# Retention and top-1 mixture of experts on one core: expert counts, ranks and table scatters at the end of the block that chose, one block's rows ahead of weight loads, squares behind the first layer

## The chip, the cores and the metric

The kernel runs on one core of a Trainium2 chip. The metric is the device time of one execution in microseconds (us). Five engines run their own instruction streams: TensorE (PE, with its weight loads as PEld), VectorE (DVE), ScalarE (ACT), GpSimd (POOL) and SyncE (SP), which here only issues DMAs.

## The reference

Two stages in a row. Retention (linear attention with a decay per head) makes 3072 token rows of 512 values; each row then goes to the one expert whose normalized embedding it matches best.

```python
# retention, B, H, S, D = 4, 8, 768, 64
for t in range(S):
    state = gamma[None, :, None, None] * state + np.einsum('bhd,bhe->bhde', k[:, :, t], v[:, :, t])
    y[:, :, t] = scale * np.einsum('bhd,bhde->bhe', q[:, :, t], state)
x = y.transpose(0, 2, 1, 3).reshape(B * S, H * D)

# top-1 experts, N, D, E, F = 3072, 512, 8, 1024
logits = xn @ en.T / tau                    # rows and embeddings divided by their norms
expert_idx = np.argmax(logits, axis=1)
gate_w = softmax(logits)[np.arange(N), expert_idx]
for e in range(E):
    mask = expert_idx == e
    h = np.maximum(x[mask] @ w1[e], 0.0)
    out[mask] = gate_w[mask, None] * (h @ w2[e])
```

## The kernel before

**Stage one** walks over 12 blocks of 256 tokens (`for m in range(NM)`, `NM = 12`). In a block PE makes scores of queries and keys (`scores`, L381), DVE masks them (`masks`, L401), PE adds the product with the carried state (`inter`) and with the values (`intra`, L445), ACT copies the result out as `yT` (`take`), and DVE turns it into token rows that SP writes to the DRAM tensor `xd` (`rows`, L472 and L479). GpSimd scales the keys and queries of the block after next (`scale_k`, L344 and `scale_q`, L339; two instructions each). PE turns them for the next block (L350, L368).

**The choice of expert** is made for groups of blocks, `GROUPS = ((0,1,2),(3,4,5),(6,7),(8,),(9,10),(11,))`, in the block behind a group's last one (`done`). The steps are:

- `logits_products` and `logits_rows` (L492, L500): logits of the previous block, turned into rows;
- `sums` (PE, L510), then `choose` and `add_counts` (DVE, L520 to L550): the largest logit, the one-hot row `oh`, the running counts `cum`;
- `count` (PE, L537 to L541) and `ranks` (DVE, L557 to L561): each token's place in its expert's list, `sloti`. Behind group 3, `pad` (PE L586, DVE L587 and L589) also fills the first expert's early list up to 288 tokens;
- `place` (GpSimd, L570): one indirect DMA for 128 tokens, which scatters them into the DRAM table `tbl`.

In the code before, `count`, `ranks` and `place` of a group stand in the block behind the one that chose: `waiting = done` at a block's end, `place_ranks(waiting)` in the middle of the next block, for group 3 at the top of block 10. Scatters are handed out some to a block (`place(ready[:n])`).

**The join.** In block 10 SP reads the first 384 table entries (`early_slots`, L606, tile `tb`), and GpSimd gathers the first expert's early rows from `xd` by them (`early_gather`, L600, three indirect DMAs into `xge`). In block 11 PE turns `xge` (`turn_rows`, L617), and ACT and DVE split it into a high and a low part (`rows_T`, L624 and L625: `xh0`, `xl0`).

**Stage two** runs the eight experts. Every product is three matmuls (high x high, high x low, low x high). Weight pieces come by SP (`load_piece`, tile `raw`, four buffers), ACT makes the high part (`split_cast`, L219) and DVE the low part (`low`, L224). The first expert's first layer (96 matmuls on 288 columns, L237) is a generator: `run(n)` issues the next n, and other steps stand between such calls. Its results go through `hidden` (ACT L243, DVE L246, tiles `hh` and `hl`); the second layer (L1055) follows. `square` (ACT, L278) sums a row's squares for its gate.

**What sets the order.** All five queues run in the order in which the code issues the steps (`tc.manual_schedule`), so a step's place in the source is its place on each engine. PSUM tiles of stage one come from a ring of four banks (`pt_`): scores, logits, turned keys and queries, `sums`, `count` and `pad` take the next bank in turn, and a PE step waits until the bank's last contents have been read.

Of the kernel before, what the change touches and what calls it, by code (L numbers as in the profile page):

```python
# [28 lines left out]
NM = B * NCB  # L29
# [76 lines left out]
def retention_moe(ctx: ExitStack, tc: tile.TileContext, q, k, v, emb, tau, w1, w2, const, const16, out):  # L106
# [67 lines left out]
    def after(i, o):  # L174
        tc.add_manual_dep(i.ins, o.ins.name, SYNC, reason="pace")
# [159 lines left out]
    def scale_q(m, a, eng=nc.gpsimd):  # L335

        at = (m % NCB * 2 + a) * 8
        w = C("tq")[:, at:at + 8].unsqueeze(2).broadcast_to([P, 8, D])
        return eng.tensor_tensor(out=qs_r[:, m % 3, :, a], in0=qin[m % 3][:, a], in1=w, op=ALU.mult)  # L339
# [427 lines left out]
    waiting, ready = None, []  # L767

    def scale_ahead(m, i):
        if m + 2 < NM:  # L770
            for s in range(2):
                after(scale_k(m + 2, s), i)
            for s in range(2):
                after(scale_q(m + 2, s), i)

    def place_ranks(g):
        pr = count(g)
        run_all(ranks(g, pr))
        if span(g).stop == NBE:
            pad()  # L780
        ready.extend(range(span(g).start, span(g).stop))

    for m in range(NM):
        nxt = m + 1 < NM
        done = last_of.get(m - 1)
        if m == NM - 2:
            place_ranks(waiting)
# [12 lines left out]
        n = 2 if m < 7 else 3 if m < 8 else 4  # L800
        if m == NM - 2:
            place(ready)
            del ready[:]
# [10 lines left out]
        if m == NM - 3:  # L814
            load_piece()
            load_piece()
# [25 lines left out]
        else:  # L842
# [10 lines left out]
            if waiting is not None and m < NM - 2:  # L853
                place_ranks(waiting)
            place(ready[:n])
            del ready[:n]
            logits_rows(m - 1, logits_products(m - 1))
            if nxt:
# [15 lines left out]
                rows(m - 1, gathered if m == NM - 2 else None)  # L874
# [10 lines left out]
                intra(m, 1)  # L885
            else:
                intra(m, 0)
# [3 lines left out]
                for low in lows:  # L891
                    low()
                intra(m, 1)
                pr = count(done)
                ps = [turn_rows(xge, EROWS, kt, bank(f"pst{kt}")) for kt in range(2)]
                run_all(ranks(done, pr))
                place(range(span(done).start, span(done).stop))
        waiting = done
# [10 lines left out]
        if m == NM - 1:  # L909
            for kt in range(KT):  # L910
                rows_T(xge, EROWS, kt, slice(0, EARLY), ps[kt] if kt < 2 else None)

# [33 lines left out]
    run(11)  # L946
# [5 lines left out]
    run(21)  # L952
# [22 lines left out]
    for j, n in EROWS:  # L975
        square(xge, n, j, j)
# [4 lines left out]
    run(DF)  # L981
    ctxa.close()
# [404 lines left out]
```

## Time and profile before

| what | before |
|---|---|
| median of 3 runs | 397.76 us (397.32 to 399.26) |
| the profiled execution: its time | 396.75 us |
| the profiled execution: its span, first to last instruction | 395.0 us |
| PE busy | 384.7 us (97%) |
| DVE busy | 241.5 us (61%) |
| ACT busy | 225.6 us (57%) |
| POOL busy | 151.1 us (38%) |
| granted TensorE clock, mean | 0.997 |

Busy is the time in which an engine has an instruction running; the span is what the profile covers, and 1.8 us of the execution's time lie around it. A timeline row gives the start in us from the span's start, the time it took in us, engine, line, operation, tiles and shapes, how many instructions it merges, and in brackets the idle time before it with what ended it.

### The profile page before, as it was taken

To read this page: it belongs to the slowest core of one execution; us is meant where nothing else is said; L and a number is where in the kernel's file an instruction comes from. 1 tells how busy PE (TensorE), PEld (TensorE's weight loads), DVE (VectorE), ACT (ScalarE), POOL (GpSimd) and SP (SyncE) were. 2 spreads that over 40 slices of the span, in tenths; PEclk is the share of its full clock that TensorE was granted. 3 is DMA by queue.
4 is the path that set the end of the run, shared out by engine and by line. 5 is a ranking of instruction groups with operands and counts; after the bars stand their busy time and mean duration, and the time that the engine had idled before them with its cause. 6 is when DMAs were issued, how large, how long until landed. Compare 5 with 4: busy or idle time off the path is not lost.

```text
span 395.0 us, 9539 instructions
## 1 busy us (share of the span) xinstructions
PE 384.7 (97%) x3646; PEld 353.9 (90%) x3646; DVE 241.5 (61%) x518; ACT 225.6 (57%) x400; POOL 151.1 (38%) x171
## 2 busy tenths in 40 slices
PE   8999999999999999999999999999999999999992
PEld 4988888888879988999999999999899889999971
DVE  5565766678998569618763862865467437486300
ACT  5687787887937266537345653735755545454420
POOL 2666487788342516024402712510480161001131
PEclk9999999999999999999999999999999999999998
DMA  8999999999479788695969789696889587933121
GB/s 229 271 313 269 273 244 296 247 271 222 109 206 290 232 208 283 195 248 201 311 186 247 268 259 243 211 332 169 247 284 312 144 278 240 211 113 110 47 94 37
DMA packets 88479, 88.39 MB, mean 224 GB/s; under 512 B 10808, under 2 KB 67000, under 8 KB 88424
## 3 DMA queue, kind: packets, MB, share of 16 engines
q1 hardware_dynamic: 83176, 74.60, 67.2%
q0 software_dynamic: 5072, 13.03, 10.0%
q8 instruction: 30, 0.49, 0.5%
q14 instruction: 25, 0.20, 0.2%
q10 hardware_dynamic: 176, 0.07, 0.1%
HBM read 65.01 MB, written 18.79 MB: 212 GB/s over the span
## 4 chain that ended last, share of the span: by engine, by line
PE 91%; DVE 2%; DMA 2%; issue 2%; ACT 0%; POOL 0%; DVEq 0%; POOLq 0%; ACTq 0%
PE pst L237 12%; PE b L237 10%; PE py L1055 8%; PE py L237 8%; PE py L445 8%; PE b L381 6%; PE b L1105 6%; PE b L1055 6%; PE pst L1055 5%; PE py L1105 4%; PE b L350 3%; PE pst L415 3%; PE pst L1105 3%; PE b L368 3%; DMA raw<-in_moe_w_dram 2%
## 5 line engine op out<-in xcount | busy, mean ns | idle before, releaser
L224 DVE TENSOR_TENSOR wlo<-raw,whi 128x1024 fp32r<-128x1024 f32 x64 | 77.8, 1218 | 22.5 <-ACT whi L219 17.2
L1087 POOL DMA_INDIRECT out_dram<-og,si x28 | 29.0, 1037 | 124.4 <-ACT og L1080 58.2
L219 ACT CAST whi<-raw 128x1024 fp32r<-128x1024 f32 x64 | 66.2, 1043 | 6.6 <-DMA raw<-in_moe_w_dram 6.5
L401 DVE TENSOR_TENSOR pm<-b,mask 128x512 f32<-128x512 f32 x48 | 29.8, 684 | 18.3 <-PE b L381 18.3
L600 POOL DMA_INDIRECT xr<-xd,gi x24 | 28.9, 1206 | 17.2 <-DMA raw<-in_moe_w_dram 10.0
L1036 DVE STREAM_TRANSPOSE xt<-xg 128x384 f32<-128x384 f32 (+1 forms) x28 | 15.7, 578 | 32.0 <-DMA xg<-xs 31.9
L237 PE MATMUL pst<-xl,whi 128*128 128x380 f32 (+7 forms) x96 | 32.2, 335 | 0.0
L237 PE MATMUL pst<-xh,whi 128*128 128x380 f32 (+7 forms) x96 | 32.1, 334 | 0.0
L237 PE MATMUL pst<-xh,wlo 128*128 128x380 f32 (+7 forms) x96 | 32.0, 333 | 0.0
L344 POOL TENSOR_TENSOR hl<-wlo,cst 128x512 f32<-128x512 f32 x22 | 22.5, 1043 | 19.8 <-DMA wlo<-in_k_dram 12.8
L1037 ACT CAST xh<-xt 128x408 fp32r<-128x408 f32 (+6 forms) x28 | 14.2, 510 | 25.1 <-DVE xt L1036 24.8
L570 POOL DMA_INDIRECT tbl<-zt,sloti x24 | 23.9, 996 | 11.1 <-issue 4.8
L263 POOL TENSOR_TENSOR r<-r,half 128x4 f32<-128x4 f32 (+1 forms) x9 | 8.9, 993 | 49.5 <-DVE r L262 49.5
L237 PE MATMUL b<-xh,whi 128*128 128x408 f32 (+7 forms) x80 | 26.8, 335 | 0.0
L237 PE MATMUL b<-xl,whi 128*128 128x408 f32 (+7 forms) x80 | 26.7, 334 | 0.0
L237 PE MATMUL b<-xh,wlo 128*128 128x408 f32 (+7 forms) x80 | 26.6, 333 | 0.0
L237 PE MATMUL py<-xh,whi 128*128 128x288 f32 (+7 forms) x80 | 26.4, 329 | 0.0
L237 PE MATMUL py<-xh,wlo 128*128 128x288 f32 (+7 forms) x80 | 26.2, 328 | 0.0
L237 PE MATMUL py<-xl,whi 128*128 128x288 f32 (+7 forms) x80 | 26.2, 327 | 0.0
L243 ACT ACTIVATE hh<-pst 128x380 fp32r<-128x380 f32 (+7 forms) x24 | 11.6, 485 | 24.5 <-PE pst L237 24.4
L381 PE MATMUL b<-qT,kT 64*128 64x128 f32 x384 | 25.3, 279 | 0.0
L381 PEld LDWEIGHTS b<-qT,kT 64*128 64x128 f32 x384 | 22.9, 188 | 1.9 <-issue 1.0
(221 smaller groups left out, 1042.1 us busy)
## 6 DMA issues: line engine op xcount, KB each, us to landing
raw<-in_moe_w_dram SPq DMA_DIRECT2D x60, 512.0 KB, 6.0
whi<-in_q_dram SPq DMA_DIRECT2D x24, 256.0 KB, 3.9
xd<-x SPq DMA_DIRECT2D x48, 128.0 KB, 3.5
wlo<-in_k_dram SPq DMA_DIRECT2D x11, 512.0 KB
xs<-xr SPq DMA_DIRECT2D x6, 768.0 KB
whi<-in_v_dram SPq DMA_DIRECT2D x6, 512.0 KB, 5.7
wlo<-in_v_dram SPq DMA_DIRECT2D x6, 512.0 KB
xg<-xs SPq DMA_DIRECT2D x16, 192.0 KB, 6.5
```

The costliest lines, as they stand in the source:

```text
L219: nc.scalar.copy(out=hv, in_=rv)
L224: eng.tensor_tensor(out=lv, in0=rv, in1=hv.bitcast(F32), op=ALU.subtract)
L237: nc.tensor.matmul(acc[:, :w], a[:, f], x[:, kt, cols], start=(n == 0), stop=(n == 3 * KT - 1))
L344: return eng.tensor_tensor(out=ks_r[:, m % 3, s, h], in0=kin[m % 3][:, h, s], in1=w[:, h], op=ALU.mult)
L381: nc.tensor.matmul(psc[a][:, j], kTs[m][a * D:(a + 1) * D, j, u].rearrange("p s c -> p (s c)"), q_cols(m, a, j, u), start=True, stop=True, ...
L401: o.append(nc.vector.tensor_tensor(out=pm, in0=psc[a], in1=w, op=ALU.mult))
L445: nc.tensor.matmul(pys[m][b][o * D:(o + 1) * D, j], lhsT, rhs, start=first, stop=True, skip_group_check=True)
L570: i = nc.gpsimd.indirect_dma_start(out=tbl[:, :], out_offset=bass.IndirectOffsetOnAxis(ap=sloti[:, n:n + 1], axis=0), in_=zt[:, n], in_off ...
L600: return nc.gpsimd.indirect_dma_start(out=xr[:n, j, :], out_offset=None, in_=xd[:rows_, :], in_offset=bass.IndirectOffsetOnAxis(ap=gi[:n, ...
L1055: nc.tensor.matmul(acc[:, :c], a[:, f], x[:, kt, :c], start=(n == 0), stop=(n == 3 * FT - 1))
L1087: i = nc.gpsimd.indirect_dma_start(out=out[:, :], out_offset=bass.IndirectOffsetOnAxis(ap=si[:n, e, j:j + 1], axis=0), in_=og[:n, j, :], i ...
L1105: nc.tensor.matmul(acc[:s, :], x[:, kt, at], a, start=(n == 0), stop=(n == 3 * FT - 1))
```

## The change

Four moves; no arithmetic is added or left out.

1. `count` and `ranks` of groups 0 to 3 move from the next block to the end of the block that chose, behind the last `intra`, and scatters follow there: `place_ready({6: 2, 8: 5}.get(m))` (for m = 9: all that are left).
2. `rows(8)` stands in block 9 ahead of the loads of weight pieces 2 and 3, and no longer behind `add_counts`.
3. In block 11 the low part of weight piece 2 stands ahead of the choice, that of piece 3 behind the split of `xge`; `count`, `ranks` and `place` of group 4 go behind that. 14 matmuls of the first layer are issued ahead of the next `sums`, where 11 were, and 18 behind it, where 21 were.
4. The three squares of `xge` go behind the first layer.

```diff
     for m in range(NM):
...
-        if m == NM - 2:
-            place_ranks(waiting)
...
-        n = 2 if m < 7 else 3 if m < 8 else 4
-        if m == NM - 2:
-            place(ready)
-            del ready[:]
...
         if m == NM - 3:
+            rows(m - 1)
             load_piece()
             load_piece()
...
-            if waiting is not None and m < NM - 2:
-                place_ranks(waiting)
-            place(ready[:n])
-            del ready[:n]
+            if m < NM - 3:
+                place_ready(3 if m == 7 else 2)
             logits_rows(m - 1, logits_products(m - 1))
...
-                rows(m - 1, gathered if m == NM - 2 else None)
+                if m != NM - 3:
+                    rows(m - 1, gathered if m == NM - 2 else None)
...
                 intra(m, 0)
                 intra(m, 1)
+                if done is not None:
+                    place_ranks(done)
+                    if m > 3:
+                        place_ready({6: 2, 8: 5}.get(m))
             else:
+                lows[0]()
                 intra(m, 0)
                 z = sums(done)
                 run_all(choose(done, z))
                 run_all(add_counts(done))
-                for low in lows:
-                    low()
                 intra(m, 1)
-                pr = count(done)
                 ps = [turn_rows(xge, EROWS, kt, bank(f"pst{kt}")) for kt in range(2)]
-                run_all(ranks(done, pr))
-                place(range(span(done).start, span(done).stop))
-        waiting = done
...
         if m == NM - 1:
             for kt in range(KT):
                 rows_T(xge, EROWS, kt, slice(0, EARLY), ps[kt] if kt < 2 else None)
+            lows[1]()
+            pr = count(done)
+            run_all(ranks(done, pr))
+            place(range(span(done).start, span(done).stop))
...
-    run(11)
+    run(14)
     low = split_cast()
     z = sums(g)
...
-    run(21)
+    run(18)
     pr = count(g)
...
-    for j, n in EROWS:
-        square(xge, n, j, j)
     run(12)
     split()
     load_piece()
     load_piece()
     run(DF)
+    for j, n in EROWS:
+        square(xge, n, j, j)
```

**GpSimd, from block 8 to the gather.** `hl` and `hh` are the keys and queries that it scales, `tbl` the table, `xge` the early rows. Before:

```order
L570 DMA tbl<-zt,sloti 25600x16 x3
L344 TENSOR_TENSOR hl<-wlo,cst_60 128x512 x2
L339 TENSOR_TENSOR hh<-whi,cst_60 128x8x64 x2
L570 DMA tbl<-zt,sloti 25600x16 x6
L600 DMA xge<-xd,tb 128x512 x2
```

In the changed kernel:

```order
L570 DMA tbl<-zt,sloti 25600x16 x5
L344 TENSOR_TENSOR hl<-wlo,cst_60 128x512 x2
L339 TENSOR_TENSOR hh<-whi,cst_60 128x8x64 x2
L570 DMA tbl<-zt,sloti 25600x16 x2
L600 DMA xge<-xd,tb 128x512 x2
```

Four scatters (group 2's) move from behind block 9's four scaling steps to ahead of them; two (group 3's) stay behind.

**SP, block 8 to block 10.** Before:

```order
L479 DMA xd<-x 256x1x128 x4
L192 DMA raw<-in_moe_w_dram 32x1024 x16
L479 DMA xd<-x 256x1x128 x4
L606 DMA tb<-tbl 128x3x10
L479 DMA xd<-x 256x1x128 x4
```

In the changed kernel:

```order
L479 DMA xd<-x 256x1x128 x4
L192 DMA raw<-in_moe_w_dram 32x1024 x8
L479 DMA xd<-x 256x1x128 x4
L192 DMA raw<-in_moe_w_dram 32x1024 x8
L606 DMA tb<-tbl 128x3x10
```

The second L479 row (block 8's token rows) stands between the halves of the weight loads; the read of the table now follows a weight load, not those rows.

**DVE in block 11**, from the counts of group 4 to block 11's logits (`xl` is the low part of `xge`, `rs`, `rank` and `sloti` the ranks, `wlo` a weight piece's low part). Before:

```order
L550 TENSOR_TENSOR cum<-cum,sm 128x8
L224 TENSOR_TENSOR wlo<-raw,whi 128x1024 x2
L557 TENSOR_TENSOR rs<-b_2169,oh 128x32
L559 TENSOR_REDUCE rank<-rs 128x4
L561 SCALAR_TENSOR_TENSOR sloti<-wmn,rank 128x4
L625 TENSOR_TENSOR xl<-pst_2175,xh 128x288
L625 TENSOR_TENSOR xl<-pst_2179,xh 128x288
L625 TENSOR_TENSOR xl<-b_2207,xh 128x288
L625 TENSOR_TENSOR xl<-b_2213,xh 128x288
L500 STREAM_TRANSPOSE parts<-b_2221 128x256
```

In the changed kernel:

```order
L550 TENSOR_TENSOR cum<-cum,sm 128x8
L625 TENSOR_TENSOR xl<-pst_2168,xh 128x288
L625 TENSOR_TENSOR xl<-pst_2172,xh 128x288
L625 TENSOR_TENSOR xl<-b_2184,xh 128x288
L625 TENSOR_TENSOR xl<-b_2190,xh 128x288
L224 TENSOR_TENSOR wlo<-raw,whi 128x1024
L557 TENSOR_TENSOR rs<-b_2197,oh 128x32
L559 TENSOR_REDUCE rank<-rs 128x4
L561 SCALAR_TENSOR_TENSOR sloti<-wmn,rank 128x4
L500 STREAM_TRANSPOSE parts<-b_2221 128x256
```

The split of `xge` moves ahead of one L224 and the ranks; the other L224 has gone up to ahead of the choice, outside these rows.

## Rows read from the trace of the kernel before

**Rows 1.** The page: busy time, share of the span and instructions by engine.
```profile
PE 384.7 (97%) x3646; PEld 353.9 (90%) x3646; DVE 241.5 (61%) x518; ACT 225.6 (57%) x400; POOL 151.1 (38%) x171
```

**Rows 2.** Waits of PE: line, what it waited for, us, times, longest.
```profile
PE pst L617 <- DMA xge<-xd,tb: 0.7, 2, 0.4
PE pst L1055 <- DVE hl L246: 0.5, 1, 0.5
```

**Rows 3.** Timeline of PE: the scores that open block 9 and block 10.
```profile
85.12 2.06 PE L381 MATMUL b<-qT,kT 64*128 64x128 f32 x32
...
93.58 2.52 PE L381 MATMUL b<-qT,kT 64*128 64x128 f32 x32
```

**Rows 4.** Timeline of PE, from the end of block 11 into the first layer.
```profile
108.23 0.19 PE L537 MATMUL b<-cum,ones 128*128 128x32 f16 x1
...
108.59 0.31 PE L617 MATMUL pst<-ident,xge 128*128 128x128 f32 x1
...
109.94 0.79 PE L617 MATMUL pst<-ident,xge 32*128 32x32 f32 x4 [0.28 <-DMA xge<-xd,tb]
...
111.74 0.64 PE L492 MATMUL b<-yT,enT 128*32 128x256 f32 x8
112.31 0.40 PE L237 MATMUL py<-xh,whi 128*128 128x288 f32 x1
...
113.97 0.25 PE L510 MATMUL b<-parts,cst 128*32 128x16 f32 x8
114.16 0.41 PE L237 MATMUL py<-xh,wlo 128*128 128x288 f32 x1
```

**Rows 5.** Timeline of DVE, block 9 and the top of block 10.
```profile
89.40 0.80 DVE L561 SCALAR_TENSOR_TENSOR sloti<-wmn,rank 128x4 int32<-128x4 f32 x1
...
92.06 0.17 DVE L525 SCALAR_TENSOR_TENSOR w<-zt,cst 128x16 f32<-128x16 f32 x1
...
94.67 0.16 DVE L561 SCALAR_TENSOR_TENSOR sloti<-wmn,rank 128x2 int32<-128x2 f32 x1
94.74 0.15 DVE L587 TENSOR_SCALAR ex<-b 128x1 f32<-128x1 f32 x1
```

**Rows 6.** Timeline of POOL, blocks 9 to 11.
```profile
89.15 2.04 POOL L339 TENSOR_TENSOR hh<-whi,cst 128x512 f32<-128x512 f32 x2
91.35 1.02 POOL L570 DMA_INDIRECT tbl<-zt,sloti  x1 [0.16 <-DVE s L433]
...
97.79 0.97 POOL L570 DMA_INDIRECT tbl<-zt,sloti  x1 [0.30 <-issue]
104.31 1.06 POOL L600 DMA_INDIRECT xge<-xd,tb  x1 [5.54 <-issue]
```

**Rows 7.** Timeline of SP's issues, blocks 8 to 10.
```profile
87.24 9.08 SPq L192 DMA_DIRECT2D raw<-in_moe_w_dram  x16
...
101.49 0.39 SPq L606 DMA_DIRECT2D tb<-tbl  x1
```

**Rows 8.** Timeline of DVE, block 11.
```profile
106.22 0.44 DVE L500 STREAM_TRANSPOSE parts<-b 128x256 f32<-128x256 f32 x1
...
108.92 2.36 DVE L224 TENSOR_TENSOR wlo<-raw,whi 128x1024 fp32r<-128x1024 f32 x2
...
113.18 0.44 DVE L500 STREAM_TRANSPOSE parts<-b 128x256 f32<-128x256 f32 x1
```

**Rows 9.** Timelines of PE and ACT, where the first expert's second layer begins.
```profile
125.79 0.30 PE L1055 MATMUL pst<-hh,whi 128*128 128x288 f32 x1
...
128.19 0.29 PE L1055 MATMUL pst<-hh,whi 128*128 128x288 f32 x1
129.00 0.40 PE L1055 MATMUL pst<-hl,whi 128*128 128x288 f32 x1 [0.52 <-DVE hl L246]
...
123.86 0.63 ACT L278 ACTIVATE sq<-xge 128x512 bf16<-128x512 f32 x1
...
126.00 0.38 ACT L243 ACTIVATE hh<-b 128x288 fp32r<-128x288 f32 x1
```

More of the change, by code (lines that the diff above doesn't have):

```diff
@@ L766, in retention_moe @@
     last_of = {ms[-1]: g for g, ms in enumerate(GROUPS)}
-    waiting, ready = None, []
+    ready = []
     def scale_ahead(m, i):
@@ L774, in scale_ahead, with place_ready @@
                 after(scale_q(m + 2, s), i)
+    def place_ready(n):
+        place(ready[:n])
+        del ready[:n]
     def place_ranks(g):
```

## The prediction

> **What bounds the kernel now.** The page's first part comes first: PE is busy for 97% of the span [rows 1], every other engine for 61% or less. So only time in which PE stands, or works on nothing new, can be won. The list of waits, for PE alone, says where that is [rows 2]: it stands 0.7 us for the gathered early rows and 0.5 us for a low part of the hidden layer. Both lie between block 11 and the start of the first expert's second layer; behind that point the chain of waits stays on PE up to the last product. Whatever PE wins or loses by then reaches the end of the kernel whole.
>
> The timeline of PE shows two more places. The scores that open block 10 take 2.52 us where those of block 9 take 2.06 [rows 3]: 0.46 us in which PE waits inside the step for a PSUM bank. And the stop for the hidden layer is larger than its wait says: 18 products take 125.79 to 128.19, 0.133 each, so the next was due at 128.32 and started at 129.00 [rows 9]. That is 0.7 us. Together 0.46 + 0.7 + 0.7 = 1.9 us can be won, 0.5% of the time; 0.5% is also about what a measurement here tells from no change.
>
> **Counts, ranks and scatters at the block's end.** PE issues the same products elsewhere; I cost them at nothing, and the three rank steps of DVE fall where it waits for the next scores anyway. What counts is GpSimd's queue. Before, the scatters of group 2 and 3 run in a row, 91.35 to 97.79 for the starts of the first and the sixth, 1.29 apart [rows 6]. They stand behind four scaling steps, of which the last two are L339 at 89.15, 2.04 for both. Now group 2's four scatters go first. Its ranks follow the end of block 8 (scores of block 9 start at 85.12 [rows 3]), so I put the first scatter at 86.2, and the four end at 86.2 + 4 x 1.29 = 91.3. The four scaling steps (4 x 1.02 = 4.1) then run 91.3 to 95.4, and the two scatters of group 3 start at 95.6 and 96.9. The last one starts 0.9 us earlier than at 97.79.
>
> The scaling steps now lie beside group 3's choice, whose step `w` stood at 92.06. The same rows show what this can cost [rows 5]. `sloti` at 89.40 took 0.80 us and ended at 90.20, which is where the first of GpSimd's two L339 ends (89.15 + 1.02); at 94.67, beside scatters, it took 0.16. So this step, which reads two SBUF tiles, waited for the running GpSimd step. Four steps of the chain do so: `w`, `oh`, `cum` and `sloti`. Each may wait between nothing and 1.02 us. I take the value of the 0.80 row's kind, a wait to the end of the running step: `w` at 92.3, `oh` at 93.3, `cum` at 94.3, `sloti` at 95.4. `pad`'s product on PE needs `cum`; it stands in PE's queue ahead of block 10's scores, which then start near 94.6 instead of 93.58. Their second half needs `pad`'s bank, read by L587 behind `sloti`, before at 94.74 and now at about 95.6. They end near 96.6 instead of 96.1. PE is 0.5 us late in block 10; without any such wait it would be 0.46 early.
>
> The Trainium skill, in "SBUF — State Buffer" (section "SBUF: two separate sides"), calls the port pair that VectorE and GpSimd share an exclusive lock for a whole instruction, and counts VectorE steps with two SBUF inputs among those that need it. By that rule all four steps wait as I took them and this part of the change costs time; the rows show it for `sloti` alone. The sum below comes out the same by either, because PE waits behind it for the gather.
>
> **The gather.** The table read goes out at 101.49 [rows 7], 3.70 us behind the start of the last scatter at 97.79, and the first gather starts at 104.31 [rows 6]. With the last scatter at 96.9 the read goes out at 100.6, and each gather lands 0.9 us earlier: the third at 109.05, where PE got it at 109.94 [rows 4]. SP is free by then: the same weight loads and token rows stand ahead of the read, only interleaved.
>
> **Block 11.** PE arrives at the first turn of `xge` at 108.59 [rows 4]. It is now 0.5 late, but group 4's `count` (108.23 to 108.59, 0.36) has gone behind the turns: 108.7. It waits for the third gather to 109.05. From there the turns took 109.94 to 111.74, 1.80: done at 110.85. Then the count, 0.36, and the logits, 111.74 to 112.31, 0.57: the first layer starts near 111.8 instead of 112.31. Fourteen products at 0.133 last to 113.65.
>
> The next `sums` needs DVE's L500, which ended 113.18 + 0.44 = 113.62 before [rows 8]. DVE had two low parts (2.36), the ranks and four splits of `xge` ahead of it; the latter two took 111.28 to 113.18, 1.90. Now one low part (1.18) fills DVE's gap after L500 at 106.22, and the other stands behind the splits. Behind the last turn at 110.85 there remain the last split on ACT and DVE, the low part, the ranks and L500. At least that is 0.35 + 0.35 + 1.18 + 0.5 + 0.44 = 2.8, a split being a quarter of 1.90 less 0.5 for the ranks; with a handover between the engines for each I take 3.1: `sums` at 113.95 and the next product at 114.15. Before, the next product started at 114.16, behind 11 products [rows 4]; now 14 are done. The gain is 3 x 0.133 = **0.4 us**, and by bounds of the same steps 0.2 to 0.7.
>
> **The squares.** The three start at 123.86 on ACT and push the hidden step to 126.00 [rows 9], 2.1 us. Behind the first layer ACT has nothing due for some time, so there they are hidden; the one that waits for them is GpSimd's memset of the late rows' buffer. The hidden step then starts some 2 us earlier, unless the weight cast ahead of it on ACT still waits for its DMA. PE's stop of **0.7 us** goes. If that cast is late, between nothing and 0.7 remains; I take the whole, since 2.1 is three times the stop.
>
> **Block 8's rows ahead of the loads.** DVE's turn of them, two steps, leaves the stretch between `cum` and the ranks of group 3, and its transfers leave the place just ahead of the table read. I count this within the numbers above; alone it is worth nothing to PE.
>
> **The sum.** -0.4 - 0.7 = -1.1 us. The profiled execution took 396.75, so a like one takes 395.65. The median of the runs shown is 1.0 higher, 397.76, and from it I forecast **396.7 us**.
>
> **Rivals.**
> - *Even.* The gather lands when it did, at 109.94, since some other step (SP's queue, the receipt of the scatters) sets the read at 101.49. Then the first layer starts at 112.7 and the product behind `sums` at 115.05 with 14 done, 0.5 later net; with the squares' 0.7 the kernel gains 0.2, and loses 0.5 if the weight cast is late too: 397.6 to 398.3. For it speaks that the read's release is one wait and everything hangs on it; against it that 97.79 + 3.70 fits the scatter alone.
> - *Slower.* The table read now follows weight loads on SP's queue. Sixteen of them took 9.08 us to issue [rows 7], so eight are worth 4.5 of traffic; if the read waits in turn behind part of it, its entries come late. The point from which this decides is a third gather later than 110.2, 1.15 behind my value: then the 1.1 is gone. At 2.1 us behind my value, 111.15, the time is 397.76 - 1.1 + 2.1 = 398.8. The row of the read at 101.49 stands on a queue whose last entries were token rows, and no row shows a read behind weights. The Trainium skill, "DMA: Bandwidth & Descriptors" (section "Queues, rings and completion order"), says that each DMA engine takes a ring's descriptors in the order in which they stand; by that rule this rival holds as far as weights are still in the ring at 100.6.
> - *All of it.* No step of the choice waits for GpSimd, or scatters start earlier, and the gather is there when PE comes: 0.46 + 0.7 + 0.7 = 1.9 gained, 395.9. Against it: GpSimd's own queue sets the last scatter, whatever PE does.
>
> **How the numbers follow.** Chances: forecast 0.47, even 0.23, all of it 0.15, slower 0.15. The range reaches from 395.6 (all of it, with 0.3 for the spread of runs) to 398.4 (even, and half of the slower case); it leaves out under 2 in 10. Faster by over 0.5% is below 395.77: half of "all of it" and the fast edge of the forecast, 0.14. Slower by over 0.5% is above 399.75: the far end of the slower case, 0.06. Within: 0.80.
>
> **What would show it.** Right: the table read near 100.6; no wait of PE at L1055 (now L1056); 14 products ahead of `sums` with the next one near 114.15; `oh` and `cum` of group 3 stretched beside L339 and L344, and block 10's scores starting near 94.6. Wrong: a third gather later than 109.94, a PE wait for `hl` that stays, or a new PE wait of over 0.5 us at `sums` or `count`. Any of these turns the gain into nothing or a loss. A new wait behind the first expert would too, since I count every product there as unchanged.

## The result and the profile after

| | before | the change |
|---|---|---|
| median of 7 runs each | 397.73 us (396.85 to 399.26) | 399.78 us (398.37 to 401.95) |
| ratio to before | 1 | 1.0055, interval 1.0036 to 1.0074 |
| the profiled execution: time, span | 396.75, 395.0 us | 401.95, 400.2 us |

The change makes the kernel 0.55% slower, some 2 us, where a gain of 1.1 us was forecast. Measured twice more against other runs of the kernel before, it gave 1.0075 (1.0042 to 1.0109) and 1.0046 (1.0021 to 1.0072).

The page's first part for the change shows nothing of it: PE is still busy for 96% of the span, against 97% [rows 1].

```profile
PE 385.9 (96%) x3646; PEld 354.5 (89%) x3646; DVE 243.0 (61%) x518; ACT 225.7 (56%) x400; POOL 154.4 (39%) x171
```

The list of PE's waits does. Columns as in [rows 2]: line, what it waited for, us in total, times, longest. The two waits of before, for `xge` and `hl`, are gone; in their place stands one of 2.1 us for `oh`, the one-hot rows of group 3, and smaller ones further back.

```profile
PE b L539 <- DVE oh L530: 2.1, 1, 2.1
...
PE pst L237 <- DVE wlo L224: 0.6, 1, 0.6
PE b L1128 <- issue: 0.5, 1, 0.5
...
PE pst L237 <- DVE xl L1044: 0.3, 1, 0.3
PE b L586 <- DVE cum L550: 0.2, 1, 0.2
PE b L510 <- DVE parts L500: 0.2, 1, 0.2
```

**The stop.** Timelines of POOL, DVE and PE of the change, end of block 9. GpSimd's four scaling steps run from 92.27 to 96.31. DVE's `w` starts in the first of them and ends behind the last: 3.15 us, where it took 0.17 before [rows 5]. PE has issued the first product of `count` and stands for `oh` until 96.82. Behind that the scores of block 10 take 3.52 us, against 2.52 [rows 3].

```profile
92.27 2.06 POOL L344 TENSOR_TENSOR hl<-wlo,cst 128x512 f32<-128x512 f32 x2
94.27 2.04 POOL L339 TENSOR_TENSOR hh<-whi,cst 128x512 f32<-128x512 f32 x2
...
93.20 3.15 DVE L525 SCALAR_TENSOR_TENSOR w<-zt,cst 128x16 f32<-128x16 f32 x1
...
94.54 0.18 PE L537 MATMUL b<-cum,ones 128*128 128x16 f16 x1
96.82 0.17 PE L539 MATMUL b<-oh,tri 128*128 128x16 f16 x1 [2.09 <-DVE oh L530]
...
97.33 3.52 PE L381 MATMUL b<-qT,kT 64*128 64x128 f32 x32
```

Busy time by stretch of the same profile; the third column from the end, PEclk, is the granted TensorE clock (1.00 is 2.4 GHz). In the stretch with the stop PE is busy for 0.91 of 3 us. Behind it the clock falls to its lower level, 1.2 GHz, for some 3.4 us, although PE is busy again without a break.

```profile
core 0: us, PE busy (x) PEld busy (x) DVE busy (x) ACT busy (x) POOL busy (x), PEclk, DMA share, GB/s
94.00:97.00 3.00, 0.91 (x15) 0.58 (x11) 2.87 (x4) 2.28 (x4) 2.31 (x3) 1.00 0.87 210
97.00:98.00 1.00, 0.78 (x10) 0.76 (x11) 0.87 (x6) 0.96 (x3) 0.07 (x1) 0.83 0.97 211
98.00:101.00 3.00, 3.00 (x32) 2.78 (x32) 1.86 (x5) 1.73 (x2) 1.92 (x2) 0.50 0.87 236
101.00:102.00 1.00, 1.00 (x38) 1.00 (x36) 1.00 (x2) 0.00 (x0) 0.00 (x0) 0.96 0.96 206
```

**The gather.** Timelines of POOL, SP and PE of the change, blocks 10 and 11. The last scatter starts 12.80 us behind block 9's scores (99.25 - 86.45), before 12.67 (97.79 - 85.12): nothing won. But PE now comes so late that it finds all of `xge` there: no wait stands at its turns.

```profile
99.25 0.97 POOL L570 DMA_INDIRECT tbl<-zt,sloti  x1 [0.31 <-DMA raw<-in_moe_w_dram]
106.79 1.79 POOL L600 DMA_INDIRECT xge<-xd,tb  x1 [6.57 <-issue]
...
103.91 0.39 SPq L606 DMA_DIRECT2D tb<-tbl  x1
...
113.10 1.16 PE L617 MATMUL pst<-ident,xge 128*128 128x128 f32 x6
114.18 1.16 PE L617 MATMUL b<-ident,xge 128*128 128x128 f32 x6
...
116.05 0.40 PE L237 MATMUL py<-xh,whi 128*128 128x288 f32 x1
...
118.64 0.40 PE L237 MATMUL py<-xh,wlo 128*128 128x288 f32 x1
```

Timeline of PE of the kernel before, the last turns of `xge`:

```profile
110.66 1.16 PE L617 MATMUL b<-ident,xge 128*128 128x128 f32 x6
```

**Behind the first layer.** Timelines of POOL, SP, PE and DVE of the change. The scatters of groups 4 and 5 end late, the last one starting at 125.74; the read of the table for the next rows (L971) goes out behind it at 130.55. PE stands 0.49 us at the turn of the first expert's late rows. The profile names nothing for it (`issue`), but their gather started 4.0 us earlier (135.31), where before it started 5.3 us ahead of the same turn (130.03 to 135.36). DVE waits for the second expert's rows (`xg`).

```profile
123.53 1.91 POOL L570 DMA_INDIRECT tbl<-zt,sloti  x1 [0.30 <-DVE hl L246]
125.74 0.97 POOL L570 DMA_INDIRECT tbl<-zt,sloti  x1 [0.30 <-issue]
...
130.55 0.34 SPq L971 DMA_DIRECT2D tb<-tbl  x1
...
139.32 0.63 PE L1128 MATMUL b<-ident,xr 128*128 128x128 f32 x4 [0.49 <-issue]
...
153.42 1.11 DVE L1037 STREAM_TRANSPOSE xt<-xg 128x416 f32<-128x416 f32 x2 [0.21 <-DMA xg<-xs]
```

**A ledger.** The table cuts the profiled span of each kernel at five starts on PE's timeline: the scores of block 9, those of block 11, the first product of the first expert's first layer, the first of its second layer, and the turn of its late rows. Each entry is the difference of two such starts, the last one that of the span and the last start. Only what follows block 9's scores is compared: their own start differs from one execution to the next (84.8 to 87.2), mostly at the kernel's beginning, where the first scores start between 8.5 and 9.6. Blocks 3 to 8, in which the steps of groups 0 to 2 moved, take 50.37 us in the change and 50.26 before. The rows below the third are experiments.

| profile | blocks 9, 10 | to first layer | first layer | second, to late rows | to the end | sum |
|---|---|---|---|---|---|---|
| before | 17.24 | 9.95 | 13.48 | 9.57 | 259.64 | 309.88 |
| the change | 20.77 | 8.83 | 13.82 | 9.45 | 260.88 | 313.75 |
| the change, another run (e13) | 20.79 | 8.83 | 13.82 | 8.80 | 260.15 | 312.39 |
| scaling first (e1) | 16.56 | 10.69 | 13.69 | 9.89 | 261.99 | 312.82 |
| stop filled (e12) | 19.19 | 9.62 | 13.69 | 9.56 | 260.95 | 313.01 |
| scaling first, group 4 early (e10) | 16.56 | 11.03 | 14.33 | 8.80 | 259.69 | 310.41 |
| scaling first, block 11 old (e15) | 16.55 | 10.32 | 14.76 | 8.80 | 259.67 | 310.10 |
| part 1 alone (e6) | 20.02 | 8.96 | 14.24 | 9.52 | 259.69 | 312.43 |
| block 11 alone (e5) | 17.24 | 14.05 | 15.28 | 8.80 | 259.66 | 315.03 |
| block 11 alone, another run (e14) | 17.24 | 9.64 | 13.68 | 10.83 | 259.66 | 311.05 |
| squares alone (e17) | 17.23 | 9.37 | 15.27 | 8.80 | 260.97 | 311.64 |

For the change against before it reads: 3.5 us lost in blocks 9 and 10, 1.1 won back where PE no longer waits for `xge`, 0.3 lost in the first layer, 0.1 to 0.8 won where it no longer waits for `hl`, 0.5 to 1.2 lost behind that. The sum is 2.5 us in one run and 3.9 in the other; the medians, in which the kernel before has waits of its own, differ by 2.0.

### The profile page after: what moved, and what is told of

Read it like the earlier page. It is cut to its first block, busy times and chain, and to the rows that moved or that the text cites. A ratio compares the mean times of both kernels' runs of the same rounds, so it can differ in the third digit from the quotient of the medians.

```text
span 400.2 us, 9539 instructions
## 1 busy us (share of the span) xinstructions
PE 385.9 (96%) x3646; PEld 354.5 (89%) x3646; DVE 243.0 (61%) x518; ACT 225.7 (56%) x400; POOL 154.4 (39%) x171
## 4 chain that ended last, share of the span: by engine, by line
PE 75%; DMA 8%; DVE 6%; SPq 3%; issue 3%; ACT 2%; POOL 2%; DVEq 0%; POOLq 0%; ACTq 0%
PE pst L237 10%; PE b L237 9%; PE py L445 8%; PE py L237 7%; PE b L381 6%; PE b L1106 6%; PE py L1056 5%; PE py L1106 4%; PE b L1056 4%; PE pst L1056 3%; PE b L350 3%; PE pst L415 3%; DMA xg<-xs 3%; PE b L368 2%; SPq L1068 2%
## 5 line engine op out<-in xcount | busy, mean ns | idle before, releaser
L224 DVE TENSOR_TENSOR wlo<-raw,whi 128x1024 fp32r<-128x1024 f32 x64 | 77.9, 1219 | 18.4 <-ACT whi L219 13.5
L600 POOL DMA_INDIRECT xr<-xd,gi x24 | 30.1, 1256 | 17.2 <-ACT sq L278 9.9
L570 POOL DMA_INDIRECT tbl<-zt,sloti x24 | 24.8, 1035 | 16.6 <-DVE sloti L561 9.6
L381 PE MATMUL b<-qT,kT 64*128 64x128 f32 x384 | 26.3, 289 | 0.0
L381 PEld LDWEIGHTS b<-qT,kT 64*128 64x128 f32 x384 | 23.9, 197 | 1.3 <-issue 0.7
```

Of the source, the lines that this page charges most:

```text
L224: eng.tensor_tensor(out=lv, in0=rv, in1=hv.bitcast(F32), op=ALU.subtract)
L381: nc.tensor.matmul(psc[a][:, j], kTs[m][a * D:(a + 1) * D, j, u].rearrange("p s c -> p (s c)"), q_cols(m, a, j, u), start=True, stop=True, ...
L570: i = nc.gpsimd.indirect_dma_start(out=tbl[:, :], out_offset=bass.IndirectOffsetOnAxis(ap=sloti[:, n:n + 1], axis=0), in_=zt[:, n], in_off ...
L600: return nc.gpsimd.indirect_dma_start(out=xr[:n, j, :], out_offset=None, in_=xd[:rows_, :], in_offset=bass.IndirectOffsetOnAxis(ap=gi[:n, ...
```

## The experiments

Theory: the stop for `oh` costs the time. Four scaling steps of GpSimd lie beside group 3's choice, DVE's `w` waits for all of them, PE for DVE, and the lower clock follows. Rival: the time goes in block 11, whose scatters now come 6 us later.

### The stop: scaling first, and half of the scaling

The first experiment is the change with the four scaling steps of block 9 ahead of group 2's scatters, as in the kernel before.

```diff
-            if m < NM - 3:
-                place_ready(3 if m == 7 else 2)
+            if m < NM - 2:
+                place_ready({7: 3, 9: 4}.get(m, 2))
...
-                        place_ready({6: 2, 8: 5}.get(m))
+                        place_ready({6: 2, 8: 1}.get(m))
```

> The changed kernel, but GpSimd's four scaling steps of block 9 stand ahead of group 2's four scatters again, as before. Theory 1 (lock): VectorE's step w of group 3's choice waits out the run of scaling steps, PE stands 2.1 us for it and then runs at 1.2 GHz. Then w takes 0.2 us here, not 3.15, the scores of block 10 about 2.0 us, not 3.5, and the time is 3 us below the changed kernel, near 396.7 (ratio to before 0.997). Theory 2 (block 11): the loss comes from group 4's scatters, which now start 6 us later and hold back the first expert's followers. Then the time stays near 399.5, whatever w does.

The second is the change without `scale_q` for block 11, so that two scaling steps lie beside the choice where there were four. Block 11's queries are left unscaled in it, so rows go to other experts and overflow their lists: only its trace up to block 11 can be read, not its time.

```diff
-            for s in range(2):
+            for s in range(2 if m != NM - 3 else 0):
                 after(scale_q(m + 2, s), i)
```

> The changed kernel; block 9 leaves out the scaling of block 11's queries (two of GpSimd's four steps), so block 11's output is not computed from its own queries. Theory 1: w waits to the end of the run that is left, so it takes about 1.1 us, not 3.15; PE stands about 0.1 to 0.3 us and keeps 2.4 GHz; the time is 397 to 397.5. If w waits only for the step that runs when it comes, it takes 0.2 to 1.0 in both kernels and the time is unchanged. Theory 2: the time stays near 399.5.

Timelines of DVE and PE of e1: `w` takes 0.17, and the scores of block 10 start 8.25 behind those of block 9 (85.58) and take 2.06.

```profile
92.30 0.17 DVE L525 SCALAR_TENSOR_TENSOR w<-zt,cst 128x16 f32<-128x16 f32 x1
...
93.83 2.06 PE L381 MATMUL b<-qT,kT 64*128 64x128 f32 x32
```

Timelines of POOL and DVE of e2: `w` ends at 93.31, just behind the second and last scaling step (93.27).

```profile
91.20 2.07 POOL L344 TENSOR_TENSOR hl<-wlo,cst 128x512 f32<-128x512 f32 x2
...
92.12 1.19 DVE L525 SCALAR_TENSOR_TENSOR w<-zt,cst 128x16 f32<-128x16 f32 x1
```

No, two and four scaling steps beside it: `w` takes 0.17, 1.19 and 3.15 us, and each time ends behind the last of them. The cause of the stop is shown. Its price is not what the theory said (3 us): e1 measured 399.67 us, 1.0027 (1.0003 to 1.0051), against 1.0055 for the change. Blocks 9 and 10 are 4.2 us shorter than in the change, but only about 1 us of that reaches the end. The blocks are also 0.7 us shorter than before (16.56 against 17.24), so what part 1 was to save on PE is there. The ledger says where it goes: PE waits again for the gathered rows, now 1.6 us, and later at the late rows, for `xl` and for a weight's low part.

```profile
106.50 1.23 DVE L224 TENSOR_TENSOR wlo<-raw,whi 128x1024 fp32r<-128x1024 f32 x1
...
106.96 1.57 POOL L600 DMA_INDIRECT xge<-xd,tb  x1 [0.31 <-issue]
...
109.35 0.33 PE L617 MATMUL pst<-ident,xge 128*128 128x128 f32 x1 [1.01 <-DMA xge<-xd,tb]
110.24 0.79 PE L617 MATMUL pst<-ident,xge 32*128 32x32 f32 x4 [0.56 <-DMA xge<-xd,tb]
...
136.41 0.63 PE L1128 MATMUL b<-ident,xr 128*128 128x128 f32 x4 [0.90 <-issue]
...
151.40 1.10 DVE L1037 STREAM_TRANSPOSE xt<-xg 128x416 f32<-128x416 f32 x2 [1.09 <-DMA xg<-xs]
```

These rows of e1 (DVE, POOL, PE, DVE) also show a price of block 11's new order: the low part that now stands ahead of the choice, 106.50 to 107.73, lies beside the third gather step, which takes 1.57 us in place of 0.93 (before, 106.98).

### The parts alone

Part 1 alone: counts, ranks and scatters at the block's end, the rest as before.

```diff
-        if m == NM - 2:
-            place_ranks(waiting)
...
-            if waiting is not None and m < NM - 2:
-                place_ranks(waiting)
-            place(ready[:n])
-            del ready[:n]
+            if m < NM - 3:
+                place_ready(3 if m == 7 else 2)
...
+                if done is not None:
+                    place_ranks(done)
+                    if m > 3:
+                        place_ready({6: 2, 8: 5}.get(m))
```

> The kernel before with counts, ranks and scatters at the block's end alone; rows, block 11 and squares as before. Theory 1: w is held for about 3 us, PE's clock falls behind the stop, and the time is 2 to 3 us above before (ratio 1.005 to 1.008). Theory 2: within 0.5 us of before (ratio 0.999 to 1.001).

402.15 us median of 6 runs, 1.0114 (1.0073 to 1.0154): the stop is there, 2.12 us in the profile, and alone it costs more than the whole change. Why it costs more is open; with 6 runs the interval is wide. The profile is of an execution of 399.26 us with a mean granted clock of 0.997; the other five have 0.983 to 0.992. So the ledger's row for e6 is that of a stop without the lower clock. Block 10's scores still take 2.88 us in it at full clock: on DVE block 8's rows (1.31 us) stand between the choice and the ranks there, since their move is not in this kernel.

Block 11 as in the change, the rest as before, and later the same once more.

```diff
+                lows[0]()
                 intra(m, 0)
...
-                for low in lows:
-                    low()
                 intra(m, 1)
-                pr = count(done)
...
-                run_all(ranks(done, pr))
-                place(range(span(done).start, span(done).stop))
...
+            lows[1]()
+            pr = count(done)
+            run_all(ranks(done, pr))
+            place(range(span(done).start, span(done).stop))
...
-    run(11)
+    run(14)
...
-    run(21)
+    run(18)
```

> The kernel before with the moves of block 11 alone (low parts, group 4's counts behind the split, 14 and 18 products). Theory 1: between no change and a gain of 0.4 us (ratio 0.999 to 1.0). Theory 2: slower by 1.5 us or more (ratio above 1.004), with the table read for experts 1 and 2 waiting for group 4's and 5's scatters.

> The kernel before with block 11 as in the change, a second time. If the reordering costs something of its own (scatters of group 4 six us later, the low part beside the third gather step): 1.002 to 1.005 again. If the first measurement was the spread of the table read and the clock behind it: 0.998 to 1.001.

399.57 us, 1.0035 (1.0014 to 1.0056), then 399.10 us, 1.0021 (0.9992 to 1.0050). It wins nothing, and if anything loses up to 0.3%. The profile of e14 has neither a late gather nor a lower clock before the end, and its waits at the second layer have grown to 1.1 us (0.9 for `hl`, 0.2 for `hh`), where before has 0.5 [rows 2]. That of e5 says little: its PE waited 3.2 us for `xge`, because the table read took 4.5 us to reach the gather (SP and POOL of e5) where before it took 2.8. That part of the table's path stands ahead of all that block 11 changes.

```profile
102.48 0.39 SPq L606 DMA_DIRECT2D tb<-tbl  x1
...
106.99 1.06 POOL L600 DMA_INDIRECT xge<-xd,tb  x1 [7.99 <-issue]
```

Its halves: only the count, ranks and scatters of group 4 behind the split of `xge` (the diff), and only the rest, the low parts and the 14 and 18 products, with group 4's steps in their old place.

```diff
-                pr = count(done)
                 ps = [turn_rows(xge, EROWS, kt, bank(f"pst{kt}")) for kt in range(2)]
-                run_all(ranks(done, pr))
-                place(range(span(done).start, span(done).stop))
...
                 rows_T(xge, EROWS, kt, slice(0, EARLY), ps[kt] if kt < 2 else None)
+            pr = count(done)
+            run_all(ranks(done, pr))
+            place(range(span(done).start, span(done).stop))
```

> The kernel before with count, ranks and scatters of group 4 (blocks 9 and 10) behind the split of the first expert's rows, and nothing else of block 11. Theory of the late scatters: the four scatters start some 4 to 6 us later, the table read for the next experts' rows waits for them, these rows and their low parts come late, and TensorE waits there: 399.0 to 399.6 us, ratio 1.003. Rival (the order of the low parts and of the 14 and 18 matmuls costs it): this one stays at 397.8 to 398.3 us.

> The other half: the kernel before with block 11's low parts and the 14 and 18 matmuls moved as in the change, but count, ranks and scatters of group 4 in their old place. Theory of the late scatters: 397.6 to 398.0 us (the step behind the turned rows wins 0.4 us at most). Rival (the order of low parts and matmuls costs it): 399.0 to 399.6 us, with a wait of TensorE for the gathered rows or for a low part of 1 us or more.

398.25 us, 0.9990 (0.9967 to 1.0013), and 399.19 us, 1.0010 (0.9983 to 1.0037). Neither half shows a cost by itself. The late scatters alone cost 0.13% at most by their interval, so the rival in its plain form falls. The other half's interval reaches 0.37% and leaves open whether the order of low parts and products costs something. The profile of e9 has the wait for `xge` of over 1 us that its rival named (3.3 us), but it is of an execution of 402.96 us, with a table read of 4.5 us (103.17 to 107.69), as in e5.

The squares behind the first layer alone, twice, and block 8's rows ahead of the loads alone.

```diff
-    for j, n in EROWS:
-        square(xge, n, j, j)
...
     run(DF)
+    for j, n in EROWS:
+        square(xge, n, j, j)
```

> The kernel before with the three squares of the first expert's rows behind its first layer, and nothing else. Squares theory: the 0.5 us that TensorE waits for the hidden low part at the start of the second layer goes, with what follows it, 0.7 us in all: 397.3 us against 398.0, ratio 0.998. Rival: the squares only push a later weight part on ScalarE, and the wait comes back at the second expert: 398.0 us, no difference.

> The kernel before with the squares behind the first layer, a second time. If the first layer runs at the higher clock: no wait for the hidden low part, second layer to late rows 8.8 us in place of 9.57, and 0.997 to 0.999 over the runs. If the spread of the gathered rows and the clock covers it in most executions: 0.999 to 1.001.

> The kernel before with block 8's rows ahead of the loads of weight pieces 2 and 3 and of the choice of group 3, nothing else. As predicted: nothing alone, 0.998 to 1.002. Rival (VectorE's 1.3 us of turning ahead of the choice make the choice, the scatters and the gather later): the last scatter no later than before only if the scatters wait for GpSimd anyway; otherwise 1.002 to 1.004 with a wait for the gathered rows above 1 us.

Squares: 398.18 and 397.97 us, 0.9997 both times (0.9967 to 1.0027, 0.9971 to 1.0023). The wait for `hl` is gone in both profiles: 8.80 us from the second layer to the late rows, before 9.57. The runs do not show the 0.8. In the profile of e17 the first layer ran at 1.2 GHz for part of its length and took 15.27, and PE stood 0.69 us at the fourth expert's weights, as in the change and in e1 (0.55 and 0.61). DVE makes those weights' low part behind the turn of the fourth expert's rows, for which it waited 9.38 us, and 7.12 before (DVE and PE of e17):

```profile
216.06 1.10 DVE L1036 STREAM_TRANSPOSE xt<-xg 128x416 f32<-128x416 f32 x2 [9.38 <-DMA xg<-xs]
...
226.00 0.45 PE L237 MATMUL pst<-xh,wlo 128*128 128x392 f32 x1 [0.69 <-DVE wlo L224]
```

Rows of block 8 ahead: 398.57 us, 1.0013 (0.9997 to 1.0029): nothing, as forecast, or a very small loss. Its profile, of an execution of 403.03 us, has the wait for `xge` of over 1 us that the rival named (3.3 us), with a table read of 4.3 us; the median does not show it.

### A staircase, and the clock

The next kernels take the change back in steps: scaling first (s1); with it group 4's count, ranks and scatters in their old place (e10, s2); with it all of block 11 as before (s3, e15), which leaves part 1 with the scaling first, block 8's rows and the squares. s0 and e13 are the change itself.

```diff
                 intra(m, 1)
+                pr = count(done)
                 ps = [turn_rows(xge, EROWS, kt, bank(f"pst{kt}")) for kt in range(2)]
+                run_all(ranks(done, pr))
+                place(range(span(done).start, span(done).stop))
...
             lows[1]()
-            pr = count(done)
-            run_all(ranks(done, pr))
-            place(range(span(done).start, span(done).stop))
```

> The whole change with two repairs: GpSimd's four scaling steps of block 9 ahead of group 2's scatters, as in the first experiment, and group 4's count, ranks and scatters back in their old place. Theory of the late scatters: the first experiment's 399.7 us less 1.2 to 1.6 us, with the squares' 0.7 us kept: 397.0 to 397.6 us, just under the kernel before. Rival (order of low parts and matmuls, or table and gather made late by the extra scatters ahead of them): 399 to 400 us as in the first experiment, with the wait for gathered rows of 1 us or more still there.

> The changed kernel once more, as the first step of a staircase on one chip. Both theories: 1.004 to 1.007 of the kernel before, about 400 us; DVE's w of group 3 takes 3 us beside GpSimd's four scaling steps, TensorE stands 2.1 us for oh. It also shows whether the half clock behind that stop comes in every execution.

> Second step: the scaling steps ahead of the scatters, block 11 as in the change. Theory of three costs (the stop for oh, group 4's late scatters, the low part beside the gather): the first of them goes, 1.0 to 1.4 us less than the change: ratio 1.002 to 1.004. Rival (the stop for oh was all of it): 0.998 to 0.999.

> Third step: group 4's count, ranks and scatters back in their old place as well. Theory of three costs: another 0.8 to 1.2 us less, ratio 1.000 to 1.001; the wait for the gathered rows of 0.6 us or more is still there, since DVE's low part of weight piece 2 still starts just ahead of the third gather step, which takes 1.6 us in place of 0.93. Rival (late scatters cost nothing, as they did alone): the same as the second step, 1.003.

> Fourth step: all of block 11 as before, with the 11 and 21 products; of the change there stay the ranks and scatters at the block's end (behind the scaling steps), block 8's rows ahead and the squares behind. Theory of three costs: the third gather step is back at 0.93 us and 0.8 us earlier than before, TensorE waits for it less than 0.3 us: ratio 0.996 to 0.998, 396.7 to 397.5 us where the kernel before takes 398. Rival (the table read waits for the scatter's landing and the gather is no earlier; nothing is won): 1.000, with 0.7 us of wait for the gathered rows as before.

> The change, beside the other three on one chip: 1.004 to 1.008 of the kernel before. Stop for oh of 2.1 us with scores of about 3.5 us behind it, if the weights and rows come as in the first profile.

> The change without block 11 and with the scaling steps ahead of the scatters, a second time. If the gather won 0.8 us and the squares 0.7 us are kept: 0.996 to 0.998. If the table read's spread and the clock swallow them: 0.999 to 1.001.

| kernel | median us | ratio to before in the same measurement |
|---|---|---|
| the change: s0, e13 | 408.40, 400.40 | 1.0075 (1.0042 to 1.0109), 1.0046 (1.0021 to 1.0072) |
| scaling first: e1, s1 | 399.67, 405.40 | 1.0027 (1.0003 to 1.0051), 1.0000 (0.9967 to 1.0032) |
| and group 4 early: e10, s2 | 398.71, 405.11 | 1.0001 (0.9965 to 1.0037), 0.9987 (0.9961 to 1.0013) |
| and block 11 old: s3, e15 | 405.59, 398.39 | 0.9994 (0.9964 to 1.0023), 1.0008 (0.9978 to 1.0037) |

In the measurement of s0 to s3 the kernel before itself took 405.49 us. In s0's profile PE stood some 3 us in block 9, in the products of keys and values (L415), and the profile names nothing that it waited for; `w` came behind the scaling and took 0.18, so this profile does not show the stop. The clock fell to 1.2 GHz behind those 3 us too (0.50 from 98 to 100). What slowed that measurement is open, and so is how much of the change's 0.75% in it belongs to the stop for `oh`; the ratios are against the kernel before in the same measurement. Scaling first takes 0.3 to 0.75% back. The mean granted clock of the executions goes the same way in that measurement: at most 0.993 in all twelve of s0, at least 0.995 in seven of the twelve of s1. Group 4's old place takes another 0.1 to 0.3%, within the intervals; the profiles are clearer, 261.99 us from the late rows to the end in e1, 259.69 in e10, though 0.9 of these 2.3 lie at the fourth expert's weights. With both repairs the kernel is level with the one before. No version beats it.

The last experiment fills PE's stop: 15 turns of the identity matrix, which nobody reads, ahead of group 3's `count`, otherwise the change.

```diff
         pr = pt_()
+        if g == 3:
+            for j in range(15):
+                nc.tensor.transpose(pr[:, j % 4 * P:(j % 4 + 1) * P], ident, ident)
```

> The change with 15 turns of the identity matrix (0.13 us each, about 2 us, into the bank that count fills afterwards) ahead of group 3's count, where TensorE otherwise stands idle for oh; nothing reads them. Clock theory: the stop keeps its length, block 10's scores still start 2.2 us late, but they take 2.06 us and not 3.52, and the granted clock stays at its higher level: 1.0 to 1.6 us less than the change in the same runs. Rival (the idle stop as such has no sequel that matters): the same time as the change, and scores above 3 us with the lower clock behind them although TensorE was busy.

Timelines of DVE and PE of e12, and its busy time by stretch: `w` still takes 2.88 us, PE works on turns meanwhile, the clock stays at 1.00, and block 10's scores take 2.06.

```profile
91.81 2.88 DVE L525 SCALAR_TENSOR_TENSOR w<-zt,cst 128x16 f32<-128x16 f32 x1
...
93.15 1.86 PE L539 MATMUL b<-ident 128*128 128x128 f32 x15
95.67 2.06 PE L381 MATMUL b<-qT,kT 64*128 64x128 f32 x32
...
98.00:101.00 3.00, 3.00 (x75) 2.52 (x68) 2.02 (x5) 0.40 (x2) 0.57 (x1) 1.00 0.73 193
```

So where PE has work in the stop, the clock stays up, and that is worth 1.6 us: 19.19 in blocks 9 and 10 against 20.77 and 20.79. One profile alone would not show it, since that of part 1 kept the clock behind an idle stop; but the granted clock of the twelve executions agrees, with a median of 0.995 against 0.992 for the change in the same measurement (e13). Yet the median is 401.76 us, 1.0076 (1.0039 to 1.0112), not below the change in the same measurement (400.40). In the profile the 1.6, and more, is given back at three places, against e13: 0.8 before the first layer (a wait for `xge` of 0.5 is there again), 0.8 before the late rows (a stop of 0.6 at them), 0.8 behind them. And in an execution in which PE reaches `count` behind the scaling steps, as in s0, the turns come on top; how often that was so the runs do not tell.

## Why the prediction was wrong

- **`w`, "a wait to the end of the running step".** This is the step that failed. The forecast took the 0.80 us of `sloti` [rows 5] as the kind of wait each of four steps has, one GpSimd step at a time: `w` at 92.3, `oh` at 93.3, `cum` at 94.3, `sloti` at 95.4. `w` waited for the whole row of scaling steps instead, once and for 3.15 us, and the steps behind it waited for nothing (0.16 to 0.17 each). Block 10's scores were to start 9.48 behind those of block 9 (94.6 - 85.12) and started 10.88 behind. The bounds were also too narrow: with a wait of 0 to 1.02 for each step, no case let one step wait for the whole row. The forecast also hid PE's 0.5 us behind the wait for the gather; the 3.5 us of blocks 9 and 10 outlast that wait, and the gather was there when PE came. The Trainium skill, "SBUF — State Buffer" (section "SBUF: two separate sides"), has whichever of VectorE and GpSimd starts first hold the pair for the whole instruction while the other blocks; the trace agrees for a running instruction, but here the next three GpSimd instructions also got in ahead of the waiting DVE step (3.15 us for steps of 1.02).
- **What a stop of PE costs.** The forecast added idle time alone. The clock at 1.2 GHz behind the stop was worth 1.6 us in the profiles of the change and of e13, beside 2.1 and 1.9 for the stop itself. Rows of before could not show it: there the granted clock is 0.997 over the whole span.
- **The last scatter 0.9 earlier.** It was not (12.80 against 12.67), since group 3's scatters waited for ranks that came late. With the scaling first it starts 1.3 earlier (96.96 - 85.58 = 11.38), the table read 1.1 earlier, the gather only 0.5, because the read then took 3.45 us to reach the gather and not 2.82. In the change nobody waits for the gather, so this term was lost without a cost: *Even* and *Slower* both put the harm at the gather, and neither is what happened. Whether weights ahead of the table read delay it (*Slower*) stays open: from the read to the gather it took 2.9 to 4.3 us in the profiles with weights next ahead of it, 2.8 to 4.5 in those with token rows.
- **Block 11, 0.4 us.** Not there. From the end of the last turn to the product behind `sums` the change took 3.30 us (115.34 to 118.64), just as forecast (110.85 to 114.15); before, it was 2.34 (111.82 to 114.16). The three products more that are done by then are 0.40 of the 0.96, and group 4's `count` about 0.2. So the new order by itself loses some 0.3 us, which is the ledger's 13.82 against 13.48 in the first layer. The 0.4 was the 0.9 of the earlier gather less such a loss (0.5 in *Even*), and the gather's 0.9 was worth nothing to a late PE. In e1, where PE did wait for the gather, the low part ahead of the choice lengthened a gather step besides (0.93 to 1.57).
- **The squares, 0.7 us.** The mechanism is right: the wait went in each profile, 0.77 us. Its worth over the runs is nil (0.9997 twice). The row of before [rows 9] is one execution with a first layer at 2.4 GHz; in the profiles of e3, e8, e10, e15 and e17 part of that layer ran at 1.2 GHz, and in e8, with the squares in their old place, the wait was hidden too (8.80 us). How often that was so over the runs is not shown.
- **"Behind that point every product is unchanged."** The second false step. The scatters of groups 4 and 5 feed a chain of its own: table read, late rows, the second expert's rows. Before, PE did not wait for it. With the scatters behind the split of `xge` and PE earlier by the squares, it does: 259.64 us from the late rows to the end became 260.15 to 261.99 in the four profiles of the ledger that have both. Two places make up nearly all of that. Between the turn of the late rows and the second expert's first layer 0.3 us are lost in the change, 0.5 in e13, 1.2 in e1 and in e12 and 0.8 in s1; nothing in s0, the one profile with both moves that does not show it. Nothing is lost there with the late scatters alone (e5, e14, e8), nor with early ones and the squares (e3, e10, e15, e17, s2, s3). So in these profiles late scatters cost time where PE is early as well; the times of the runs agree with it and are too wide to show it. The second place is the fourth expert's weights: 0.8 us in the change, 0.9 in e1, and all of the 1.3 of e17, which has early scatters. So that loss is not the scatters' doing, and why the fourth expert's rows come late in these executions is open.

The first reading, "whatever PE wins by then reaches the end whole", was the root of the last two. PE is busy for 97%, but chains through GpSimd and the DMA queues run beside it with little slack, so PE's gains up to the first layer are worth what those chains let through, and a loss is partly covered by waits that go: the 3.5 us of the stop and the clock behind it became 2 in the medians.

## What to carry to other kernels

A DVE step of two SBUF inputs that is put beside a row of GpSimd steps should be costed at up to the length of the whole row, and a stop of PE at its length plus what the lower clock may take behind it. When a change makes the busiest engine earlier, look at the waits that were just hidden on the other chains before counting the gain: here blocks that became 4.2 us shorter were worth about 1 to 3 us. And before a GpSimd step is moved, ask which DVE steps it will then lie beside, in both directions.

## What the runs showed of the hardware

- DVE's `w` (128x16, two SBUF inputs) beside none, two and four GpSimd steps of 1.02 us: 0.17, 1.19 and 3.15 us, each time to the end of the row. `sloti` (128x4) at 89.40 got in after one step [rows 5], with another L339 step still to come. What decides between the two is open.
- The other way round, GpSimd's indirect steps lengthen beside DVE's two-input low parts: a gather step of 1.57 us (e1), one of 1.79 and a scatter of 1.91 (both in the change), where most take 0.93 to 1.06. In these three the low part had started first (for the scatter at 123.38, 0.15 us ahead of it). A scatter of before that started 0.16 us ahead of a low part took 0.97 (119.46 and 119.62).
- A PE stop of 2.1 us was followed by some 3.4 us at 1.2 GHz with PE busy (the change; in e13 behind a stop of 1.9); the same stop filled with turns was not. In the profile of part 1 alone the same stop of 2.12 us had no lower clock behind it, and 4 of the 12 executions of e13 have a mean granted clock of 0.996 or 0.997, so it does not follow every time.
- The table read took 2.8 to 4.5 us from its issue to the first gather that uses it, in profiles whose code up to there is the same (before 101.49 to 104.31, e5 102.48 to 106.99). This spread of 1.7 us is larger than every gain that was forecast, and in e5 the clock was at 1.2 GHz for some 10 us from the wait for `xge` on (about 110.7 to 120.9).
